# Attention and a routed layer on one core: rows of ten units by transposing DMAs, and a new written order

## Chip, cores, metric

The kernel runs on one core of a Trainium2 chip. The metric is the device time in microseconds (us) of one execution.

## What is computed

```python
scores = (1.0 / np.sqrt(64)) * np.matmul(q, k.transpose(0, 1, 3, 2))   # q, k, v: 8 x 12 x 448 x 64
attn = np.maximum(scores, 0.0) ** 2 / 448
x = np.matmul(attn, v)                    # then heads side by side: 8 x 448 x 768
for b in range(8):
    s = x[b] @ w_gate                     # one score for each of 448 rows
    top = np.argpartition(-s, 128)[:128]  # the 128 rows with the highest scores
    h = np.maximum(x[b, top] @ w1, 0.0)   # 768 x 1024
    out[b] = x[b]
    out[b, top] += (1.0 / (1.0 + np.exp(-s[top])))[:, None] * (h @ w2)
```

## The kernel before

The attention is cut into 24 units, each with four heads of one batch; three units make a batch (unit u belongs to batch u // 3). The engines are PE (TensorE, matrix products), ACT (ScalarE), DVE (VectorE), POOL (GpSimd, which here mainly issues DMAs) and SP (which issues the first loads and the transposing DMAs).

A unit goes through these steps. `L` (line 106) loads q, k and v of the unit with a cast to bf16, from POOL, into one of six buffers each. `T` (226) turns queries (w=0) and keys (w=1) on PE, and `TE` (240) copies them out of PSUM on DVE. `SC`, called `S` in the order (256), makes the scores of one of seven blocks of keys in a pair of PSUM banks; `R` (264) clamps them at zero on ACT into `r_sb`; `Q` (270) squares three or four blocks at once on DVE into `a_sb`. `V` (276) multiplies with the values over the seven blocks, and `X` (286) copies the result, scaled, on ACT or DVE into `xT_sb`, which holds features on partitions and tokens along the row; three such buffers go round by batch. The rows of the output need the opposite layout. Two ways lead there:

- `RT` (298) turns a unit on PE, by eight matmuls of 128 columns of weights or, with by64=1, sixteen of 64, and `RE` (307) copies the turned rows from PSUM into `x_rows` on DVE or ACT.
- `XB` (314) has SP issue two DMAs that transpose from `xT_sb` straight into `x_rows`, each over 128 partitions. Units in the list `BYDMA` (45), 15 to 20, go this way. So that a block of 128 partitions holds two neighbouring heads, `L` loads these units by two DMAs of 64 partitions each for q, k and v (line 115), where other units have one DMA of 128 (line 111).

`ST` (324) stores a batch's `x_rows` to the output from POOL by two DMAs. It has to wait for all three units' rows, and what POOL issues after it waits behind it. Then the routed layer of the batch follows (class `Moe`, 337): scores by `colx` and `colE`, ranks by `bt`, `rk`, `cs0`, `cs` and `rank`, the choice by `hots`, `sel` and `sE`, a gather `XG` of the chosen rows by an indirect DMA on POOL, `XT` and `xeE` to turn them, `h` and `hE`, `y` and `yE` for the two products, `gs` and `sig` for the gate, and `ADD`, an accumulating indirect DMA on POOL. The last batch doesn't gather; `xe` takes its chosen rows by matmuls with `x_rows`. `bt` and the steps after it for one batch stand among the attention of later units.

The order of all work is a string written out by hand, `ORDER` (535 to 623). A loop (629) reads it item by item and calls the function of that name; an item such as `R,0,3,A` is block 3 of unit 0 on ACT. Every engine gets its instructions in this order and runs them in this order, each engine as far ahead as its semaphores let it.

At the start, SP loads the first queries and keys in fp32 (`LFq`, `LFk`), ACT and DVE cast them (`Cq`, `Ck`), PE turns the first seven blocks of queries into one PSUM bank and the first two blocks of keys into the next, and `TQE` and `TKE` copy them out. `PW` is a matmul on zeros that only keeps PE occupied.

```python
def XB(u):
    for g in range(2):
        m = 2 * uu + g
        nc.sync.dma_start_transpose(out=x_rows[b][:, :, 128 * m:128 * m + 128],
                                    in_=xT_sb[b % NX][:, m].rearrange("p c n -> p (c n)"))
```

Of the kernel before, what the change touches and what calls it, by code (L numbers as in the profile page):

```python
# [678 lines left out]
```

## Time and profile before

| what | value |
|---|---|
| median of 3 runs | 197.46 us (197.3 to 199.45) |
| profiled execution, its own time | 197.49 us |
| its span, first to last instruction | 195.8 us |
| time outside the span | 1.69 us |
| TensorE clock granted, mean over the span | 0.986 of full |

Busy time counts what an engine executes; shares are of the span. A matmul's end is modelled in the profile, so a PE that looks busy can still be held up a little. An engine's idle time is put down to what ended it. SP's own instructions and DMA issues are not counted as busy there.

### The profile page before, as it was taken

The page shows a single profiled execution, that of the slowest core. Times are in us where ns is not written, and L with a number is a line of the kernel's source. Part 1 is how long each engine was busy: PE and PEld are TensorE (multiplying, and loading weights), DVE is VectorE, ACT ScalarE, POOL GpSimd, SP SyncE. Part 2 cuts the span into 40 slices and gives each one's busy share as a digit, 9 for nine tenths or more (in the row PEclk, how much of TensorE's full clock was granted, in tenths as well). Part 3 has the DMA queues.
Part 4 walks back from the last instruction along what each step waited for, and adds up shares of the span by engine and source line. Part 5 has one row for each costly group of instructions (what it writes and reads, how often), then busy time and mean ns, then how long its engine had stood idle before and what let it go on. Part 6 is the DMA issues. An engine that isn't in the chain of part 4 may idle for free.

```text
span 195.8 us, 7321 instructions
## 1 busy us (share of the span) xinstructions
PE 178.4 (91%) x3221; PEld 125.0 (64%) x3221; DVE 162.0 (83%) x228; ACT 164.4 (84%) x209; POOL 111.1 (57%) x160
## 2 busy tenths in 40 slices
PE   7888979989999999999999989999999999999900
PEld 7545647656667676775768765677667668588700
DVE  1599999999999999999999989897997969773100
ACT  4699999999999998899999989999998886533410
POOL 7958562558735189485794987229013367423360
PEclk9999999999999999999999999999999999999995
DMA  5999999999999969999999999998999999939391
GB/s 171 148 186 203 204 209 202 263 282 194 181 197 347 207 99 172 197 299 246 174 167 191 326 149 235 252 130 115 120 133 309 155 272 216 187 79 291 47 125 26
DMA packets 32333, 37.70 MB, mean 193 GB/s; under 512 B 8744, under 2 KB 29614, under 8 KB 31278
## 3 DMA queue, kind: packets, MB, share of 16 engines
q0 software_dynamic: 24928, 34.74, 95.4%
q1 hardware_dynamic: 7374, 2.50, 10.2%
q8 instruction: 25, 0.41, 0.9%
q14 instruction: 6, 0.05, 0.1%
HBM read 42.08 MB, written 14.16 MB: 287 GB/s over the span
## 4 chain that ended last, share of the span: by engine, by line
PE 61%; ACT 25%; issue 5%; DVE 4%; POOL 2%; POOLq 0%; DVEq 0%; ACTq 0%
ACT r_sb L216 24%; PE ps L260 12%; PE ps L487 10%; PE ps L505 10%; PE ps L281 9%; PE ps L233 7%; PE ps L295 4%; PE ps L209 2%; PE ps L365 2%; POOL out_dram L523 2%; PE ps L377 1%; DVE a_sb L274 1%; ACT xT_sb L216 1%; DVE qkt L220 1%; DVE mask_sb L388 1%
## 5 line engine op out<-in xcount | busy, mean ns | idle before, releaser
L216 ACT ACTIVATE r_sb<-ps 128x896 bf16<-128x896 f32 x168 | 140.2, 967 | 6.3 <-PE ps L260 5.8
L274 DVE TENSOR_TENSOR a_sb<-r_sb 128x2688 bf16<-128x2688 bf16 (+1 forms) x48 | 84.8, 1784 | 2.7 <-ACT r_sb L216 1.8
L260 PE MATMUL ps<-qkt 64*64 64x448 bf16 x672 | 55.5, 361 | 3.2 <-ACT r_sb L216 2.3
L281 PE MATMUL ps<-a_sb,v_sb 64*64 64x448 bf16 x672 | 41.7, 350 | 0.6 <-ACT r_sb L216 0.4
L260 PEld LDWEIGHTS <-qkt 64*64 64x64 bf16 x672 | 22.1, 104 | 21.1 <-issue 11.0
L220 DVE COPY qkt<-ps 128x1792 bf16<-128x1792 bf16 (+2 forms) x25 | 26.0, 1045 | 2.1 <-PE ps L233 1.6
L281 PEld LDWEIGHTS <-v_sb 64*64 64x64 bf16 x672 | 21.4, 107 | 9.3 <-issue 1.6
L446 POOL DMA_INDIRECT xg<-out_dram,idx x7 | 13.3, 1897 | 22.3 <-DVE idx L430 12.0
L487 PE MATMUL ps<-xeT,w_sb 128*128 128x128 bf16 (+1 forms) x396 | 24.6, 220 | 0.0
L487 PEld LDWEIGHTS <-w_sb 128*128 128x128 bf16 (+1 forms) x396 | 21.9, 98 | 4.0 <-issue 3.1
L505 PE MATMUL ps<-w_sb,hT 128*128 128x384 bf16 (+1 forms) x132 | 24.3, 327 | 0.0
L523 POOL DMA_INDIRECT out_dram<-gye,idx x9 | 17.4, 1929 | 8.6 <-ACT gye L216 6.6
L327 POOL DMA_DIRECT2D out_dram<-x_rows x8 | 4.5, 561 | 28.9 <-DMA x_rows<-xT_sb 9.2
L111 POOL DMA_DIRECT2D v_sb<-in_v_dram x18 | 14.0, 781 | 4.2 <-PE ps L260 1.8
L505 PEld LDWEIGHTS <-hT 128*128 128x128 bf16 (+1 forms) x132 | 11.1, 98 | 8.0 <-issue 2.1
L233 PE MATMUL ps<-ident,q_sb 128*64 128x128 bf16 x336 | 14.3, 225 | 1.6 <-ACT r_sb L216 1.2
L233 PEld LDWEIGHTS <-q_sb 128*64 128x64 bf16 x336 | 11.8, 112 | 6.3 <-issue 5.6
L222 DVE TENSOR_SCALAR xT_sb<-ps 128x896 bf16<-128x896 f32 x12 | 13.1, 1088 | 2.1 <-PE ps L281 1.2
L111 POOL DMA_DIRECT2D q_sb<-in_q_dram x17 | 12.9, 757 | 3.0 <-DVE a_sb L274 1.2
L233 PE MATMUL ps<-ident,k_sb 128*64 128x128 bf16 x336 | 14.1, 221 | 0.0
L111 POOL DMA_DIRECT2D k_sb<-in_k_dram x17 | 12.6, 741 | 2.2 <-PE ps L260 1.4
L216 ACT ACTIVATE xT_sb<-ps 128x896 bf16<-128x896 f32 x12 | 11.7, 975 | 0.8 <-PE ps L281 0.8
(122 smaller groups left out, 200.4 us busy)
## 6 DMA issues: line engine op xcount, KB each, us to landing
out_dram<-x_rows POOLq DMA_DIRECT2D x8, 768.0 KB, 5.5
out_dram<-x_rows POOLq DMA_DIRECT2D x8, 576.0 KB, 6.6
v_sb<-in_v_dram POOLq DMA_DIRECT2D x18, 224.0 KB, 8.2
q_sb<-in_q_dram POOLq DMA_DIRECT2D x17, 224.0 KB, 9.0
k_sb<-in_k_dram POOLq DMA_DIRECT2D x17, 224.0 KB, 8.7
w_sb<-in_moe_w_dram POOLq DMA_DIRECT2D x6, 256.0 KB, 8.2
w_sb<-in_moe_w_dram POOLq DMA_DIRECT2D x8, 192.0 KB, 8.0
q_sb<-in_q_dram POOLq DMA_DIRECT2D x12, 112.0 KB, 6.2
```

The lines of the kernel that those rows point to most:

```text
L111: nc.gpsimd.dma_start(out=dst, in_=src(t, u))
L216: nc.scalar.activation(out=out_, in_=in_, func=func or AF.Copy, scale=scale)
L220: nc.vector.tensor_copy(out=out_, in_=in_)
L222: nc.vector.tensor_scalar(out=out_, in0=in_, scalar1=scale, scalar2=None, op0=ALU.mult)
L233: nc.tensor.matmul(out=PSB[HALF[j], at["T", u, w], n * 128:(n + 1) * 128], lhsT=s[:, j, c, :], rhs=ident, is_transpose=True, start=(n == 0 ...
L260: nc.tensor.matmul(out=PS[HALF[hf], bank + j, :S], lhsT=qkt[u][HALF[j], 1, c, hf, :], rhs=qkt[u][HALF[j], 0, :, hf, :], start=True, stop=True)
L274: nc.vector.tensor_tensor(out=a_sb[u][:, c0:c1], in0=r, in1=r, op=ALU.mult)
L281: nc.tensor.matmul(out=PS[HALF[j], at["V", u] + hf, :S], lhsT=v_sb[u % NBUF][HALF[hf], j, c, :], rhs=a_sb[u][HALF[hf], c, j, :], start=(c ...
L446: read = reads[self.b] = nc.gpsimd.indirect_dma_start(out=self.xg, out_offset=None, in_=out[0:self.b + 1].rearrange("b s d -> (b s) d"), i ...
L487: nc.tensor.matmul(out=PS[p, self.at["h"] + bk, o:o + 128], lhsT=w1_sb[:, m, f * 128 + p.start:f * 128 + p.stop], rhs=self.xeT[:, m, :], s ...
L505: nc.tensor.matmul(out=PS[p, self.at["y"] + w, :384], lhsT=self.hT[:, f, p], rhs=w2_sb[:, f, w * 384:(w + 1) * 384], start=(f == 0), stop= ...
L523: add = nc.gpsimd.indirect_dma_start(out=out[0:self.b + 1].rearrange("b s (w d) -> (b s w) d", w=w), out_offset=bass.IndirectOffsetOnAxis( ...
```

## The change

The units whose rows go by transposing DMAs are now ten: 21 and 22 in the old manner, by two DMAs over 128 partitions behind loads in halves (`BYDMA`), and 9, 10, 12, 13, 15, 16, 18 and 19 (`BYFOUR`) behind whole loads, by four DMAs over 64 partitions each, one for each head. Units 17 and 20 go back to PE, so `RT` and `RE` remain for 14 units where there were 18. The first five blocks of the first queries go to one PSUM bank and the last two (`TB`) to another; their copies are split between ACT (five) and DVE (two), and DVE also copies the first keys. The order string is written anew in full; steps `X`, `hE`, `xeE` and `yE` change engines in places, and `PW,7` becomes `PW,5`.

```diff
-    BYDMA = (15,16,17,18,19,20)
+    BYDMA = (21,22)
+    BYFOUR = (9,10,12,13,15,16,18,19)
+    NA = 5
...
+        if (u, w, n0) == (0, 0, 0):
+            n1 = NA
+        o = NA if (u, w, n0) == (0, 0, NA) else 0
...
+    def TB(bank):
+        at["TB"] = bank
+        T(0, 0, bank, NA, NC)
...
         for g in range(2):
             m = 2 * uu + g
-            nc.sync.dma_start_transpose(
-                out=x_rows[b][:, :, 128 * m:128 * m + 128],
-                in_=xT_sb[b % NX][:, m].rearrange("p c n -> p (c n)"))
+            if u in BYDMA:
+                nc.sync.dma_start_transpose(
+                    out=x_rows[b][:, :, 128 * m:128 * m + 128],
+                    in_=xT_sb[b % NX][:, m].rearrange("p c n -> p (c n)"))
+                continue
+            for j in range(2):
+                h = 4 * uu + 2 * j + g
+                nc.sync.dma_start_transpose(
+                    out=x_rows[b][:, :, 64 * h:64 * h + 64],
+                    in_=xT_sb[b % NX][HALF[j], m].rearrange("p c n -> p (c n)"))
...
-    Zz PW,32,0 Zi Zs LFq Cq,0 Zt LFk,0,2 Zm Ck,0,2,D Cq,1 T,0,0,0 TK,0,2 LFk,2,7 TQE,0,7,D Ck,2,7,D TKE,0,2,A
+    LFq Zz PW,32,0 Zi Zs Zh Cq,1 Zt Cq,0 T,0,0,0 TB,2 LFk,0,2 Ck,0,2,D TK,0,2 TQE,5,7,D LFk,2,7 TKE,0,2,D
+    TQE,0,5,A PW,5,3 S,0,0,2 S,0,1,4 R,0,0,A Ck,2,7,D R,0,1,A TK,2,7 Lw TKE,2,7,D Zm PW,8,6 S,0,2,0 R,0,2,A
```

SP's queue, before: all six units' transposes behind the first loads.

```order
L320 DMA_TRANSPOSE x_rows<-xT_sb_105 128x4x128 [waits DMASW4_49,DMASW5_49,DVE_49,Pool_49]
L320 DMA_TRANSPOSE x_rows<-xT_sb_105 128x4x128
L320 DMA_TRANSPOSE x_rows<-xT_sb_105 128x4x128 [waits DMAHW0_49,Activation_49]
L320 DMA_TRANSPOSE x_rows<-xT_sb_105 128x4x128 [waits DMAHW1_49]
L320 DMA_TRANSPOSE x_rows<-xT_sb_105 128x4x128 [waits DMAHW2_49,DVE_49]
L320 DMA_TRANSPOSE x_rows<-xT_sb_105 128x4x128 [waits DMAHW3_49]
```

SP's queue now, the first two units (10, then 9, both of batch 3 in the first `xT_sb` buffer).

```order
L339 DMA_TRANSPOSE x_rows_2089<-xT_sb0_103 128x4x64 [waits DMASW6_49,DMASW7_49,DVE_49,Pool_49]
L339 DMA_TRANSPOSE x_rows_2089<-xT_sb0_103 128x4x64
L339 DMA_TRANSPOSE x_rows_2089<-xT_sb0_103 128x4x64 [waits DMAHW0_49]
L339 DMA_TRANSPOSE x_rows_2089<-xT_sb0_103 128x4x64 [waits DMAHW1_49]
L339 DMA_TRANSPOSE x_rows_2089<-xT_sb0_103 128x4x64 [waits DMAHW2_49,Activation_49]
L339 DMA_TRANSPOSE x_rows_2089<-xT_sb0_103 128x4x64 [waits DMAHW3_49]
L339 DMA_TRANSPOSE x_rows_2089<-xT_sb0_103 128x4x64 [waits DMAHW4_49]
L339 DMA_TRANSPOSE x_rows_2089<-xT_sb0_103 128x4x64 [waits DMAHW5_49]
```

Twelve transposing DMAs in SP's queue have become thirty-six, 32 of them half as large, and they begin six units earlier.

POOL's queue around the store of batch 6 (two DMAs from `x_rows`) and the load of the last values, unit 23's (`v_sb_102`), before.

```order
L327 DMA out_dram<-x_rows 64x3072
L328 DMA out_dram<-x_rows 64x2304
L523 DMA out_dram<-gye,idx 1344x768
L111 DMA v_sb_102<-in_v_dram 128x2x448
L523 DMA out_dram<-gye,idx 1792x768
```

The same place now; `v_sb_100` and `v_sb_101` are the values of units 21 and 22.

```order
L117 DMA v_sb_100<-in_v_dram 64x2x448 x2
L117 DMA v_sb_101<-in_v_dram 64x2x448 x2
L465 DMA xg<-out_dram,idx 128x768
L346 DMA out_dram<-x_rows 64x3072
L347 DMA out_dram<-x_rows 64x2304
L113 DMA v_sb_102<-in_v_dram 128x2x448
```

The accumulating DMA that stood between the store and the load has moved behind; the load is still behind the store.

ACT's queue from the last `r_sb` evictions on, before (`hT`, `xeT`, `gye` are written by `hE`, `xeE`, `yE`).

```order
L216 ACTIVATE r_sb<-ps 128x896 x7
L216 ACTIVATE x_rows<-ps 128x4x256
L479 ACTIVATE g__3045<-ps 128x1
L216 ACTIVATE r_sb<-ps 128x896 x4
L216 ACTIVATE x_rows<-ps 128x4x256
L216 ACTIVATE xT_sb_104<-ps 128x2x448
L216 ACTIVATE x_rows<-ps 128x4x256
L216 ACTIVATE hT<-ps 128x1024
```

ACT's queue at the same place now.

```order
L218 ACTIVATE gye<-ps,g__2482 128x768
L218 ACTIVATE r_sb<-ps 128x896 x6
L218 ACTIVATE xT_sb_104<-ps 128x2x448
L218 ACTIVATE hT<-ps 128x1024
L218 ACTIVATE xT_sb_104<-ps 128x2x448
L218 ACTIVATE x_rows<-ps 128x4x256
```

Two of the three copies into `x_rows` (units 21 and 22) have left ACT's end; a copy into `xT_sb` and one into `hT` have come to it.

## Rows read from the trace of the kernel before

**Rows 1.** The page, part 1: busy time, share of the span, instructions.

```profile
PE 178.4 (91%) x3221; PEld 125.0 (64%) x3221; DVE 162.0 (83%) x228; ACT 164.4 (84%) x209; POOL 111.1 (57%) x160
```

**Rows 2.** Busy time by stretch: PE, PEld, DVE, ACT, POOL, granted clock, DMA share, GB/s.

```profile
10.00:70.00 60.00, 54.82 (x1062) 36.40 (x1057) 58.73 (x77) 60.00 (x75) 33.48 (x51) 1.00 1.19 222
70.00:160.00 90.00, 89.04 (x1670) 62.08 (x1667) 82.95 (x117) 85.10 (x109) 53.74 (x72) 1.00 1.15 194
160.00:186.50 26.50, 26.26 (x388) 19.93 (x385) 16.33 (x28) 13.16 (x20) 12.04 (x14) 1.00 0.77 174
```

**Rows 3.** Waits: who waited for whom, us in total, times, longest.

```profile
POOL out_dram L327 <- DMA x_rows<-xT_sb: 9.2, 1, 9.2
```

**Rows 4.** The chain that ended last: start, us, what.

```profile
73.44 0.55 PE ps L295 x8
74.00 1.30 PE ps L505 x8
...
112.52 0.47 PE ps L295 x16
...
169.81 1.48 PE ps L281 x28
...
180.50 1.34 PE ps L487 x24
```

**Rows 5.** Groups by line and shape, evictions on DVE and ACT: busy us, mean ns.

```profile
L220 DVE COPY x_rows<-ps 128x1024 bf16<-128x1024 bf16 x14 | 9.5, 684 | 0.3 <-issue 0.2
...
L216 ACT ACTIVATE xT_sb<-ps 128x896 bf16<-128x896 f32 x12 | 11.7, 975 | 0.8 <-PE ps L281 0.8
...
L216 ACT ACTIVATE x_rows<-ps 128x1024 bf16<-128x1024 bf16 x4 | 4.2, 1051 | 2.7 <-PE ps L295 2.7
...
L216 ACT ACTIVATE hT<-ps 128x1024 bf16<-128x1024 f32 x3 | 3.1, 1026 | 2.3 <-PE ps L487 2.3
...
L216 ACT ACTIVATE xeT<-ps 128x768 bf16<-128x768 bf16 x3 | 2.6, 871 | 0.0
...
L216 ACT ACTIVATE gye<-ps,g__743 128x768 f32<-128x768 f32 x1 | 0.9, 901 | 0.2 <-PE ps L505 0.2
```

**Rows 6.** Instructions on the tile x_rows: ns min/median/max, first and last start.

```profile
L320 SPq DMA_TRANSPOSE x_rows<-xT_sb x12: 1190/1276/3841, 126.0 to 154.0; - x12
```

**Rows 7.** The transposing line alone: DMA to landing.

```profile
DMA to landing us min/median/max: 3.5/4.8/9.0
```

**Rows 8.** DMA queues from 125 to 160 us: packets, MB, share of 16 engines.

```profile
q1 hardware_dynamic: 6528, 1.57, 48.1%
```

**Rows 9.** DMA issues of the whole span: count, KB each, median us to landing.

```profile
q_sb<-in_q_dram POOLq DMA_DIRECT2D x17, 224.0 KB, 9.0
...
q_sb<-in_q_dram POOLq DMA_DIRECT2D x12, 112.0 KB, 6.2
```

**Rows 10.** Groups by line on POOL: whole loads (L111) and halves (L115).

```profile
L111 POOL DMA_DIRECT2D q_sb<-in_q_dram x17 | 12.9, 757 | 3.0 <-DVE a_sb L274 1.2 <-DMA q_sb<-in_q_dram 0.8 <-PE ps L260 0.6
...
L115 POOL DMA_DIRECT2D q_sb<-in_q_dram x12 | 7.4, 635 | 0.8 <-issue 0.8
```

**Rows 11.** Timeline of the start: start us, us, what.

```profile
5.70 0.62 DVE L220 COPY qkt<-ps 128x896 bf16<-128x896 bf16 x1 [0.40 <-PE ps L233]
...
5.91 0.38 ACT L216 ACTIVATE qkt<-ps 128x256 bf16<-128x256 bf16 x1 [1.26 <-PE ps L233]
...
6.81 7.53 ACT L216 ACTIVATE r_sb<-ps 128x896 bf16<-128x896 f32 x9 [0.51 <-PE ps L260]
```

**Rows 12.** Timeline from 160 us on: last values, last r_sb, weights of last V, last DMA.

```profile
160.66 1.43 POOL L111 DMA_DIRECT2D v_sb<-in_v_dram  x1
...
164.71 3.35 ACT L216 ACTIVATE r_sb<-ps 128x896 bf16<-128x896 f32 x4 [1.62 <-PE ps L260]
...
169.74 1.12 PEld L281 LDWEIGHTS <-v_sb 64*64 64x64 bf16 x28 [0.37 <-issue]
...
188.08 1.56 POOL L523 DMA_INDIRECT out_dram<-gye,idx  x1 [0.26 <-issue]
```

More of the change, by code (lines that the diff above doesn't have):

```diff
@@ L232, in T @@
             for j in range(2):
-                nc.tensor.matmul(out=PSB[HALF[j], at["T", u, w], n * 128:(n + 1) * 128],
+                nc.tensor.matmul(out=PSB[HALF[j], bank if o else at["T", u, w], (n - o) * 128:(n - o + 1) * 128],
                                  lhsT=s[:, j, c, :], rhs=ident, is_transpose=True,
-                                 start=(n == 0), stop=(n == NC - 1), skip_group_check=True)
+                                 start=(n == o), stop=(n == n1 - 1 if (u, w) == (0, 0) else n == NC - 1),
+                                 skip_group_check=True)
+    def TB(bank):
+        at["TB"] = bank
+        T(0, 0, bank, NA, NC)
     def TK(n0, n1):
@@ L247, in TE @@
         else:
-            put(eng, flat[:, w, n0 * 128:n1 * 128], PSB[:, at["T", u, w], n0 * 128:n1 * 128])
+            own = (u, w, n0) == (0, 0, NA)
+            put(eng, flat[:, w, n0 * 128:n1 * 128],
+                PSB[:, at["TB"], :(n1 - n0) * 128] if own else PSB[:, at["T", u, w], n0 * 128:n1 * 128])
     def TQE(n0, n1, eng):
@@ L621 @@
[L621 to L622 removed]
+    LFq Zz PW,32,0 Zi Zs Zh Cq,1 Zt Cq,0 T,0,0,0 TB,2 LFk,0,2 Ck,0,2,D TK,0,2 TQE,5,7,D LFk,2,7 TKE,0,2,D
+    TQE,0,5,A PW,5,3 S,0,0,2 S,0,1,4 R,0,0,A Ck,2,7,D R,0,1,A TK,2,7 Lw TKE,2,7,D Zm PW,8,6 S,0,2,0 R,0,2,A
+    L,q,1 Zc S,0,3,2 S,0,4,6 S,0,5,4 L,k,1 Q,0,0,3 R,0,3,A R,0,4,A L,k,2 T,1,0,0 T,1,1 S,0,6,2 Zg,6 R,0,5,A
@@ new lines @@
+    W,1,3,8 V,8,5 V,8,6 X,8,A W,1,2,8 T,11,0,6 T,11,1 TE,11,2,D Zx,2 RT,6,1,2 R,10,3,A S,10,4,0 colx,2,0,3
+    colx,2,1 RE,6,D colx,2,2 colE,2 S,10,5,4 R,10,4,A W,1,6,8 S,10,6,6 S,11,0,2 W,1,1,8 R,10,5,A R,10,6,A
+    Q,9,0,3 sel,1,0 sE,1 RT,7,0,1 RE,7,D RT,8,0,4 bt,2,5 rk,2,0 RE,8,D rk,2,2 S,11,1,6 V,9,0,0 V,9,1 ST,1
+    W,1,7,8 V,9,2 R,11,0,A L,q,13 S,11,2,2 R,11,1,A V,9,3 V,9,4 V,9,5 V,9,6 R,11,2,A rk,2,3 y,0,0,2,0,6
+    y,0,1,2,0 L,k,13 rk,2,1 W,1,5,8 X,9,A S,11,3,2 R,11,3,A S,11,4,4 y,0,2,2,0 y,0,3,2,0 L,v,10 L,v,11 S,11,5,0
@@ new lines @@
+    h,1,7,0 S,13,2,4 V,11,0,6 hE,1,2,D V,11,1 S,13,3,2 V,11,2 V,11,3 V,11,4 R,13,2,A V,11,5 R,13,3,A S,13,4,0
+    R,13,4,A L,k,15 Q,12,3,7 S,13,5,4 V,11,6 X,11,A L,q,14 T,14,0,2 T,14,1 TE,14,2,D R,13,5,A y,1,0,2,1,0
+    y,1,1,2,1 y,1,2,2,1 S,13,6,6 L,v,13 Q,13,0,3 L,q,16 S,14,0,2 S,14,1,4 XB,10 y,1,3,2,0 y,1,4,2,0 R,13,6,A
+    Q,13,3,7 y,1,5,2,0 R,14,0,A y,1,6,2,0 colx,3,0,6 colx,3,1 colx,3,2 R,14,1,A gs,1,7 sig,1 L,q,15 S,14,2,2
+    R,14,2,A T,15,0,4 T,15,1 colE,3 S,14,3,6 TE,15,2,D RT,11,0,2 RE,11,D y,1,7,2,0 L,q,18 R,14,3,A bt,3,3 rk,3,3
@@ new lines @@
+    T,19,1 TE,19,2,D S,18,5,6 S,18,6,0 L,k,20 h,3,4,0 h,3,5,0 R,18,5,A h,3,6,0 h,3,7,0 R,18,6,A Q,18,3,7
+    V,17,0,6 V,17,1 V,17,2 S,19,0,0 S,19,1,4 V,17,3 V,17,4 hE,3,2,A R,19,0,A R,19,1,A S,19,2,2 R,19,2,A V,17,5
+    V,17,6 XB,15 T,20,0,0 T,20,1 X,17,D TE,20,2,D S,19,3,4 R,19,3,A S,19,4,6 colx,5,0,2 R,19,4,A colx,5,1
+    colx,5,2 sel,4,3 L,q,21 colE,5 S,20,0,0 sE,4 Q,19,0,3 S,20,1,4 bt,5,2 rk,5,2 rk,5,0 gs,3,3 R,20,0,A R,20,1,A
+    V,18,0,6 V,18,1 S,20,2,0 V,18,2 V,18,3 V,18,4 V,18,5 V,18,6 RT,17,0,4 cs0,5,5 R,20,2,A ST,4 XB,16 rk,5,1
```

158 lines of the change are left out of this document (71 added, 87 removed).

## Prediction

> **What bounds the kernel now.** I read the busy shares first, then the same by stretch, then the chain that ended last and the waits, and last the timelines of the two ends. The shares [rows 1] give PE 91%, ACT 84% and DVE 83%: no engine alone explains the time. By stretch [rows 2] they do. From 10 to 70 us ACT is busy 60.00 of 60 us, while PE has 5 us free: ACT sets the pace. From 70 to 160 us PE is busy 89.04 of 90, with ACT close behind at 85.10, so PE sets the pace and ACT has 4.9 us to spare. From 160 to 186.5 us PE is busy 26.26 of 26.5 and ACT only half the time: PE alone. [...] After PE's end there remain the last accumulating DMA, issued at 188.08 [rows 12], and its landing. DMA shares are above 1 because queues overlap, and the transfers are not what PE waits for; the one long wait on them is POOL's, 9.2 us once, for transposed rows before a store [rows 3].
>
> The profiled execution took 197.49 us against a median of 197.46, so sums made on its trace need no correction. About 1% (2 us) is what a measurement of this kernel can tell from no change.
>
> **The change part by part.**
>
> *Turns on PE.* By the order string, 18 turns become 14: of those with by64=0 13 become 10, of those with by64=1 five become four. A turn costs 0.55 us on the chain in the first form and 0.47 in the second [rows 4]. PE sheds 3 x 0.55 + 0.47 = 2.1 us. All six units that leave PE (9, 10, 12, 13, 21, 22) and both that come back (17, 20) lie behind 70 us, where PE sets the pace.
>
> *Evictions.* Counted in the two strings, ACT loses three copies to `x_rows` (3 x 1.05), three to `xeT` (3 x 0.87), and half a `gye` (0.6); it gains an `xT_sb` (0.98), two and a half `hT` (2.6) and three `gye` (3 x 0.90) [rows 5], and some 0.5 at the start and in the last `xeT`. That is 6.3 lost, 6.8 gained: +0.5 us, spread over the span, which I count at nothing. DVE sheds the other side of these moves and one copy to `x_rows` (0.68), some 6 us in all, but it bounds no stretch, so I count that at nothing.
>
> *The stretch where ACT sets the pace.* It ends near 75 us, within unit 10. The 77th `r_sb` eviction (unit 10's last) stood behind five copies to `xT_sb`; now it stands behind four and a gate of 0.2 us. That is worth 0.8 us there, if DVE, busy 58.73 of 60 us [rows 2], takes the copy without being late. Ends: 0.8 gained; or, DVE having nearly no room, nothing or some loss: a copy more of about 1.1 us on DVE, delaying the squares by that much. I take 0, in the middle.
>
> *Start.* The first scores wait for two copies in parallel, 896 columns on DVE (0.62 us, from 5.70) and 256 on ACT (0.38, from 5.91) [rows 11]. Now ACT takes 640 and DVE two of 256. ACT's need not wait for the keys' turn any more, DVE's second still does. The last to end should be DVE's, at about 5.91 plus less than 0.38, so near 6.2 instead of 6.32: 0.15 us earlier. Ends: 0.4 earlier, or 0.3 later, should ACT's 640 columns wait for the same matmuls as today and then take as long as DVE's 896. I take -0.15.
>
> *Loads.* 36 half loads become 12 and 52 whole loads become 64 on POOL: 24 x 0.635 - 12 x 0.757 = 6.2 us of POOL's time less [rows 10]. POOL is busy 57% of the span, so this shortens nothing by itself; it lets a load behind others start earlier. Bytes are the same.
>
> *Transposing DMAs.* In the 35 us from 125 on, the twelve took 48.1% of 16 engines [rows 8]: 16.8 us, or 1.40 us each, for 128 partitions of 1 KB. No row shows one of 64 partitions. Lower bound: half, as its bytes are half, so 4 x 1.40 + 32 x 0.70 = 28.0 us, 11.2 more. Upper bound: the same 1.40, 50.4 us, 33.6 more. Spread over some 85 us from unit 10's result on, that is 0.13 to 0.40 on top of a DMA share of 1.15 [rows 2]. I take the lower end: the packets in the queue's row (6528 for 12, 544 each) fit a count by 256 B of source, which halves with the partitions. On SP an issue takes 1.28 us [rows 6]; a unit's four take 5.1 where two took 2.6, and its rows are ready 3 x 1.28 + 4.8 = 8.6 us after `X`, by the median landing [rows 7], against 6.1 before. Behind unit 10's four stand unit 9's, which is ready earlier but is issued second; batch 3's store waits for both, about 14 us behind unit 10's `X`. Behind that store on POOL are the values of units 15 and 18, wanted five units later and more. I count it as hidden.
>
> [...]
>
> *Where it could bite.* The last values, unit 23's, are loaded behind batch 6's store on POOL, before and now. Before, the load went out at 160.66; with the 9.0 us of a whole load [rows 9] it lands at 169.7, and `V` of unit 23 begins at 169.74, its first weights behind a gap of 0.37 us [rows 12]: already just in time. Now the store waits for unit 19's four transposes. From unit 19's `X`: 3 x 1.28 = 3.8, the last landing 4.8, two stores' issue 1.1, the load 9.0: 18.7 us. PE's work in between by the string: 21 block steps of `V` and 18 of `S` (some 0.2 each, from 28 matmuls in 1.48 us [rows 4]), 16 groups of `h` (0.34), 8 of `y` (0.33), four `T`, five `colx`, a turn and small ones (another 4.5): near 21 us. So it is covered by about 2 us.
>
> *The end.* Behind the last `r_sb` eviction, which ended at 164.71 + 3.35 = 168.06 [rows 12], PE loses unit 22's turn (0.5) but gets four groups of `h` (1.3), four of `y` (1.3) and two gate rows of the last batch (0.4) that stood before it: 2.5 us heavier. PE has 2.1 + 2.5 = 4.6 us less before it. On ACT, before it, two copies to `x_rows` and three to `xeT` go, one `hT`, two `gye` and the start's 0.3 come: 4.7 - 3.1 = 1.6 us less. So the last eviction can come 4.6 us earlier as far as PE goes, and 1.6 plus part of ACT's spare 4.9 us as far as ACT goes.
>
> *Sum.* PE alone gives -2.1. But in the stretch before 160 us ACT hands PE its data block by block with 95% of its own time taken and no work lost, so part of what PE gains comes back as waits for `r_sb`. Ends of what is kept: all, 2.1; or none and 0.9 lost (third rival). I take half, 1.05. With the start: 197.49 - 1.05 - 0.15 = 196.3 us.
>
> **The rivals.**
>
> *All of it is kept, and the first stretch too.* PE works without a gap from 70 us on, the order fits, ACT's 0.8 us counts, and the earlier last load does no harm: 197.49 - 2.1 - 0.8 - 0.15 = 194.4. For it: PE's 98.9% from 70 to 160 [rows 2], and 6 us less on both POOL and DVE. Against it: ACT's total is unchanged.
>
> *Slower: the transposes come late.* If a DMA over 64 partitions costs 1.40 us like one over 128, unit 19's last landing rises towards the longest of today, 9.0 [rows 7], and the whole load's 9.0 with it. The mechanism is the chain above: transposes, store on POOL, last values, `V` of unit 23, with PE waiting in order behind it. It decides from a landing of about 4.8 + 2 = 7 us on; at 9.0 and a load of 12 it is 4.2 + 3 - 2 = 5 us late, one for one in the end: 196.3 + 5 = 201.3; half of it, 198.8, if only half of these two delays comes. I price it at 200.5. For it: POOL's 9.2 us wait for just such rows [rows 3]. Against it: half the bytes.
> [...]
>
> *ACT holds the end.* PE's relief before the last `r_sb` eviction is not used, ACT brings it 1.6 us earlier and no more, and the 2.5 us of added tail follow in full: 197.49 + 2.5 - 1.6 = 198.4. For it: ACT's 95%. Against it: ACT's spare time there came from waiting for PE, which now has less to do.
>
> **How the numbers follow.** Chances: forecast 0.40 (195.0 to 197.6 of its own); all kept 0.30; transposes late 0.17; ACT holds the end 0.13. Faster by over 1% (under 195.5): most of the second, 0.28, and a quarter of the first, 0.10: 0.38. Slower by over 1% (above 199.4): most of the transposes' case, 0.14, and of ACT's case and others 0.06: 0.20. Within 1%: 0.42. The range leaves 0.1 on each side: down to 193.2, somewhat under the second case, and up to 200.6, the price of the slower one.
>
> **What would show it.** Right: no PE wait for DMAs; transposes in the queue's row at about 0.7 us of 16 engines each; PE's turns fewer by 2.1 us on the chain; the last `r_sb` eviction between 164 and 166 us; `V` of unit 23 without a wait on `v_sb`; first `r_sb` at 6.65. Wrong: a transpose's landing above 7 us in the middle, PE idle ahead of unit 23's `V`, a last `r_sb` eviction later than 166.4, or ACT busy under 58 us between 10 and 70, which would mean that the new order makes it wait.

## The result, and the profile after

The changed kernel took 200.12 us in the middle of 16 runs (197.88 to 204.44), the kernel before 197.42 beside it. The ratio is 1.011, 95% interval 1.008 to 1.0141: slower by 1.1%. Forecast was 196.3; the time lies at the upper end of the range, on the wrong side of no change. Middles are of all runs, ratios of the undisturbed ones alone, and since a gap of the kind found below can by itself put a run among the disturbed, both are given. The profiled execution took 200.34 us (span 198.3).

From the page of the changed kernel: busy time (the line to [rows 1]), PE's and its granted clock's tenths in 40 slices, the queues of transposes and of instructions, the transposes' landing:

```profile
PE 178.3 (90%) x3219; PEld 123.9 (62%) x3219; DVE 155.6 (78%) x225; ACT 165.8 (84%) x209; POOL 98.5 (50%) x148
...
PE   7888999879999999999999989999999599999910
...
PEclk9999999999999999999999999999999979999985
...
q1 hardware_dynamic: 12238, 3.55, 15.5%
q8 instruction: 25, 0.41, 0.9%
...
x_rows<-xT_sb SPq DMA_TRANSPOSE x36, 7.0
```

By stretch (columns as in [rows 2]):

```profile
10.00:70.00 60.00, 54.83 (x1086) 36.85 (x1080) 58.45 (x68) 59.77 (x76) 34.54 (x54) 1.00 1.19 220
70.00:160.00 90.00, 86.29 (x1600) 59.61 (x1599) 80.34 (x111) 83.48 (x103) 38.90 (x52) 0.99 1.23 197
160.00:189.00 29.00, 29.00 (x432) 21.17 (x429) 12.18 (x29) 16.60 (x24) 12.91 (x16) 0.97 0.97 193
```

The first stretch is as before. In the second PE is idle for 3.7 us where it was idle for 1.0, and 2.2 of it stand in one slice of the page (the 5, at 154 to 159 us); the clock falls in the next one. PE's timeline there (start, us, what, and in brackets the idle time ahead and what ended it):

```profile
155.53 0.38 PE L396 MATMUL ps<-ident_f,cols 128*128 128x128 f32 x2
158.10 0.58 PE L396 MATMUL ps<-ident_f,cols 128*128 128x128 f32 x2 [2.19 <-issue]
```

and the two stretches, of the gap and behind it:

```profile
155.80:158.10 2.30, 0.11 (x1) 0.00 (x0) 0.17 (x1) 0.86 (x2) 1.08 (x1) 1.00 1.33 138
158.10:161.60 3.50, 3.50 (x26) 1.73 (x26) 1.71 (x8) 1.10 (x3) 0.00 (x0) 0.51 0.96 159
```

PE stands still for 2.2 us in the middle of four like matmuls (`bt` of batch 6), and "issue" says that it waited for nothing that the profile shows. In the kernel before the same four run on end (0.63 us):

```profile
153.56 0.63 PE L377 MATMUL ps<-ident_f,cols 128*128 128x128 f32 x4
```

Over the 3.5 us behind the gap the granted clock is 0.51 in the mean, in the gap itself 1.00; the trace's clock record has it at half of full speed for 3.4 us from 158.13 on. Eight score matmuls take 0.96 us there, and 0.57 in the kernel before, where the clock at that place was 1.00:

```profile
160.03 0.96 PE L272 MATMUL ps<-qkt 64*64 64x448 bf16 x8
```

```profile
155.13 0.57 PE L260 MATMUL ps<-qkt 64*64 64x448 bf16 x8
```

The rest of the chain: the last `r_sb` eviction, the last values' `V` (28 matmuls, no wait in brackets, as forecast) and the last accumulating DMA:

```profile
165.77 2.58 ACT L218 ACTIVATE r_sb<-ps 128x896 bf16<-128x896 f32 x3
```

```profile
170.83 1.52 PE L293 MATMUL ps<-a_sb,v_sb 64*64 64x448 bf16 x28
```

```profile
190.88 1.56 POOL L542 DMA_INDIRECT out_dram<-gye,idx  x1 [0.26 <-issue]
```

The last `r_sb` ends at 168.35, before at 168.06 [rows 12]; unit 21's last one had still been ahead by 1.66 us (149.64 against 151.30). From the last `r_sb` to the last DMA it is 22.5 us, before 20.0: the tail is 2.5 us heavier.

The chain of the slower rival did start. POOL waited for transposing DMAs ahead of a store twice, 15.3 us in all, the second time 5.1 us for unit 19's ahead of batch 6's store; that went out at 162.0 us (before 158.2) and the last values' load at 163.1 (before 160.7). PE, itself late, did not wait for them.

```profile
  POOL out_dram L346: 15.3, 2
```

```profile
162.02 0.57 POOL L346 DMA_DIRECT2D out_dram<-x_rows  x1 [5.14 <-issue]
...
163.09 0.76 POOL L113 DMA_DIRECT2D v_sb<-in_v_dram  x1
```

**What the gap is.** The page has a queue q8 of the kind "instruction": 25 packets, 0.41 MB, so 16 KB each. PE's records hold 6438 matmuls and weight loads, so one packet comes for some 256 of them. No view lists the packets singly; what follows is counted from the records of the traces (weight loads and matmuls in order of time, two instructions a pair, packets from 0). No packet starts before PE has passed some 150 to 180 places of its 256, and every gap sits at 170 to 188 places of the next 256: by these counts the packets are PE's own instructions, 256 in each, and PE seems to ask for a packet when it enters the one ahead, and needs it when that one ends. That is a reading of the counts; the asking itself is in no record: "asked for" below is the moment at which PE passes place 180, and a packet is as late as its start lies behind that. Packet 20 was asked for at 149.4 us, started only at 155.57 and landed at 156.47; PE stood from instruction 5560 (21 x 256 + 184) on until 158.10. In the kernel before the same packet started 1.05 us after it was asked for.

### The profile page after: what moved, and what is told of

Same layout as the page of the kernel before. It is cut to its first block, busy times and chain, and to the rows that moved or that the text cites. A ratio compares the mean times of both kernels' runs of the same rounds, so it can differ in the third digit from the quotient of the medians.

```text
span 198.3 us, 7363 instructions
## 1 busy us (share of the span) xinstructions
PE 178.3 (90%) x3219; PEld 123.9 (62%) x3219; DVE 155.6 (78%) x225; ACT 165.8 (84%) x209; POOL 98.5 (50%) x148
## 3 DMA queue, kind: packets, MB, share of 16 engines
q1 hardware_dynamic: 12238, 3.55, 15.5%
## 4 chain that ended last, share of the span: by engine, by line
PE 57%; ACT 20%; DVE 9%; issue 8%; POOL 2%; POOLq 0%; ACTq 0%; DVEq 0%
ACT r_sb L218 19%; PE ps L272 12%; PE ps L506 10%; PE ps L524 10%; PE ps L293 9%; PE ps L238 6%; DVE a_sb L286 3%; PE ps L307 2%; PE ps L211 2%; PE ps L384 2%; DVE qkt L222 2%; POOL out_dram L542 2%; PE ps L396 1%; DVE xT_sb L224 1%; ACT xT_sb L218 1%
## 5 line engine op out<-in xcount | busy, mean ns | idle before, releaser
L272 PE MATMUL ps<-qkt 64*64 64x448 bf16 x672 | 56.5, 363 | 4.2 <-ACT r_sb L218 1.5
L293 PE MATMUL ps<-a_sb,v_sb 64*64 64x448 bf16 x672 | 43.1, 351 | 1.3 <-issue 0.6
L272 PEld LDWEIGHTS <-qkt 64*64 64x64 bf16 x672 | 23.2, 104 | 21.4 <-issue 10.7
L524 PE MATMUL ps<-w_sb,hT 128*128 128x384 bf16 (+1 forms) x148 | 25.6, 334 | 0.1
L465 POOL DMA_INDIRECT xg<-out_dram,idx x7 | 7.6, 1085 | 34.3 <-DVE idx L449 17.0
L542 POOL DMA_INDIRECT out_dram<-gye,idx x9 | 15.2, 1684 | 9.4 <-ACT gye L218 7.7
L113 POOL DMA_DIRECT2D k_sb<-in_k_dram x21 | 15.6, 747 | 5.1 <-PE ps L272 2.5
L113 POOL DMA_DIRECT2D q_sb<-in_q_dram x21 | 15.9, 762 | 3.0 <-PE ps L272 1.2
L113 POOL DMA_DIRECT2D v_sb<-in_v_dram x22 | 16.3, 750 | 2.0 <-issue 0.7
L407 DVE SCALAR_TENSOR_TENSOR mask_sb<-ps,cols,tie 128x448 bf16<-128x448 f32 (+2 forms) x24 | 12.3, 546 | 3.5 <-PE ps L396 2.8
```

Of the source, the lines that this page charges most:

```text
L113: nc.gpsimd.dma_start(out=dst, in_=src(t, u))
L272: nc.tensor.matmul(out=PS[HALF[hf], bank + j, :S], lhsT=qkt[u][HALF[j], 1, c, hf, :], rhs=qkt[u][HALF[j], 0, :, hf, :], start=True, stop=True)
L293: nc.tensor.matmul(out=PS[HALF[j], at["V", u] + hf, :S], lhsT=v_sb[u % NBUF][HALF[hf], j, c, :], rhs=a_sb[u][HALF[hf], c, j, :], start=(c ...
L407: nc.vector.scalar_tensor_tensor(out=mask, in0=row[:, o:S], scalar=self.cols[:, c:c + 1], in1=tie[:, :S - o], op0=ALU.subtract, op1=ALU.is ...
L465: read = reads[self.b] = nc.gpsimd.indirect_dma_start(out=self.xg, out_offset=None, in_=out[0:self.b + 1].rearrange("b s d -> (b s) d"), i ...
L524: nc.tensor.matmul(out=PS[p, self.at["y"] + w, :384], lhsT=self.hT[:, f, p], rhs=w2_sb[:, f, w * 384:(w + 1) * 384], start=(f == 0), stop= ...
```

## Experiments

All times are against the kernel before in the same series. "Profiled" is the time of the execution that was profiled, which can lie far from the middle. Gaps are those above 1 us between two weight loads of PE at a packet's end, in that execution, with the packet that PE waited for in brackets; the changed kernel's own, above, is 2.3 us (20) by this measure.

| run | edit of | middle (lowest to highest), us | before | ratio [95%] | profiled, us | gaps, us (packet) |
|---|---|---|---|---|---|---|
| `again` | after, none | 200.14 (197.98 to 202.0) | 197.19 | 1.011 [1.006, 1.016] | 197.98 | 1.3 (20) |
| `ph_plus` | after | 202.17 (200.5 to 204.57) | 197.19 | 1.024 [1.020, 1.028] | 201.94 | 1.1 (8), 2.3 (20) |
| `ph_minus` | after | 200.33 (196.99 to 203.62) | 197.19 | 1.004 [1.001, 1.008] | 200.53 | 1.3 (19) |
| `bydma` | after | 202.95 (198.78 to 216.63) | 197.19 | none | 202.12 | 1.4 (8), 1.5 (19), 2.8 (20) |
| `no_t` | after | 196.79 (196.32 to 197.2) | 197.14 | 0.998 [0.996, 1.000] | 196.32 | none |
| `v22late` | after | 201.03 (199.42 to 203.02) | 197.14 | 1.016 [1.012, 1.020] | 200.25 | 2.7 (20) |
| `vearly` | after | 202.34 (198.69 to 205.36) | 197.14 | 1.012 [1.007, 1.018] | 198.69 | 1.2 (14), 1.8 (20) |
| `v23` | after | 202.27 (200.58 to 206.39) | 197.14 | 1.022 [1.018, 1.026] | 201.29 | 3.2 (20) |
| `before_plus` | before | 198.54 (197.42 to 199.34) | 197.92 | 1.001 [0.998, 1.005] | 197.50 | none |
| `by2` | after | 201.15 (199.02 to 204.65) | 197.92 | 1.008 [1.004, 1.013] | 202.94 | 2.4 (14), 1.1 (20) |
| `pe19` | after | 199.72 (198.01 to 205.56) | 197.92 | 1.004 [1.000, 1.008] | 205.56 | 4.2 (19) |
| `swap` | after | 201.79 (198.76 to 206.69) | 197.92 | 1.012 [1.007, 1.016] | 201.87 | 1.2 (14), 1.5 (17) |
| `copy` | after | 198.06 (197.12 to 200.05) | 197.87 | 1.001 [0.998, 1.004] | 197.38 | none |
| `before_dense` | before | 198.12 (197.36 to 199.41) | 197.87 | 1.000 [0.997, 1.002] | 199.41 | 1.2 (14) |
| `cand` | after | 199.31 (198.11 to 201.02) | 197.87 | 1.006 [1.003, 1.009] | 201.02 | 1.2 (14) |
| `thin` | after | 203.17 (200.91 to 205.1) | 197.87 | 1.022 [1.016, 1.027] | 203.15 | 1.1 (20) |

### Is it the instruction stream?

`again`: no edit.

> The changed kernel, unaltered, for a second look. In its first profile PE stood still from 155.91 to 158.10 us in the middle of the four matmuls at L396 with nothing to wait for, and its clock was then at the lower level until 161.5; the instruction packet fetched at 155.57 for PE was the latest of all, counted in PE instructions. Theory F (PE ran out of instructions because that packet came late, and the stand-still then cost the clock): the same gap at the same instructions, 1.5 to 3 us long, again with the packet starting at about 155 us; time 199.5 to 200.5. Theory O (the new order itself costs the time, through its heavier tail; the stand-still was chance): no gap over 1 us in this profile, and a time of 199.5 to 200.5 all the same. If the gap is missing and the time is near 197 to 198, the event is there in some executions and not in others, and F holds for the difference.

`ph_plus` and `ph_minus` cut or join the warm-up matmuls, so that everything behind them changes its place in the stream, and their columns in all nearly stay (6976 and 7041, against 7040; in `ph_plus` they take 5.3 us of PE, in the changed kernel 5.4):

```diff
-    def PW(n, bank):
+    def PW(n, bank, w):
-            nc.tensor.matmul(out=PS[:, bank, :128], lhsT=zero, rhs=zero, ...
+            nc.tensor.matmul(out=PS[:, bank, :w], lhsT=zero[:, :128], rhs=zero[:, :w], ...
-  PW,32,0      PW,5,3      PW,8,6      PW,10,7
+  PW,48,0,84   PW,10,3,64  PW,16,6,64  PW,20,7,64     (ph_plus)
+  PW,8,0,512   PW,2,3,320  PW,2,6,512  PW,3,7,427     (ph_minus)
```

> The changed kernel with its 55 warm-up matmuls before 12 us cut into 94 shorter ones of the same time in all (32 of 128 columns into 48 of 84, 23 of 128 into 46 of 64): nothing else moves, but every later instruction of PE stands 78 places later in its stream, so each packet of 256 instructions begins 78 instructions earlier in the work. Theory F: packet 20 is asked for about 2 us earlier in the work, ahead of the loads issued from 146.2 us on, and the gap at L396 goes or changes place; time 196 to 198 if no other packet comes late. Theories O and D: no change, 199.5 to 200.5, and a gap, if there is one, at the same matmuls.

> The other way: the 55 warm-up matmuls of 128 columns joined into 15 longer ones of the same time in all, so that every later instruction of PE stands 80 places earlier in its stream and each packet begins 80 instructions later in the work. Theory F: the gap at L396 goes or moves by some 80 instructions; if the packet still starts at 155.6 us, PE is then 358 instructions into the packet before and not 438, and does not run dry: 196 to 198. Theories O and D: no change, 199.5 to 200.5, and a gap, if there is one, at the same matmuls.

PE's timelines around the gap, of `again`:

```profile
155.57 0.38 PE L396 MATMUL ps<-ident_f,cols 128*128 128x128 f32 x2
157.08 0.38 PE L396 MATMUL ps<-ident_f,cols 128*128 128x128 f32 x2 [1.13 <-issue]
```

of `ph_plus`:

```profile
154.30 0.44 PE L307 MATMUL ps<-ident,xT_sb 128*128 128x128 bf16 x5
156.90 0.33 PE L307 MATMUL ps<-ident,xT_sb 128*128 128x128 bf16 x3 [2.16 <-issue]
```

and of `ph_minus`:

```profile
151.10 0.64 PE L506 MATMUL ps<-xeT,w_sb 128*64 128x128 bf16 x16
152.94 0.41 PE L506 MATMUL ps<-xeT,w_sb 128*64 128x128 bf16 x8 [1.21 <-issue]
```

The work at the gap is another each time (gate rows, a turn, the hidden layer), the place in the stream is not. Counted from the records:

| kernel | gap at PE's instruction | packet: asked for, start, landed | PE goes on |
|---|---|---|---|
| after | 5560 = 21 x 256 + 184 | 149.4, 155.57, 156.47 | 158.10 |
| `again` | 5560 | 149.4, 154.26, 155.64 | 157.08 |
| `ph_plus` | 5560 | 149.1, 154.46, 155.35 | 156.90 |
| `ph_minus` | 5304 = 20 x 256 + 184 | 145.0, 150.35, 151.37 | 152.94 |
| `no_t` | none | 149.2, 152.56, 153.45 | |

So theory F is shown in its main point: PE stops where a packet ends, with the next one not yet landed, and goes on 1.4 to 1.6 us after it has. Its guess at the times was off: a shift did not free the kernel, it moved the gap or added one (`ph_plus` has a second at 70.6 us), since packets asked for at 145.0, 149.1 and 149.4 us all came 4.8 us late or more. `again` gives the cost: beside the first profile it has 1.06 us less of a gap and no stretch at the lower clock behind it (granted from 156 to 160 us: 1.00 against 0.77; PE busy 177.0 against 178.3 us), 2.4 us in all, which is the 197.98 against 200.34. That execution was the fastest of its six; what those of 200 us and more had that were not profiled, no trace shows. Theory O falls with the next run.

### What makes the packet late?

`no_t` leaves the eight transposing DMAs of units 18 and 19 out:

```diff
     def XB(u):
+        if u in (18, 19):
+            nc.vector.memset(x_rows[b][:, :, 256 * uu:256 * uu + 256], 0.0)
+            return
```

> The changed kernel without the eight transposing DMAs of units 18 and 19: their part of the result's rows is zeros from VectorE instead, so that part of the output is left out. Nothing else moves. Theory T (the transposes share the DMA engines with the loads, which are then served late, and PE's packet 20, asked for near 149.4 us, stands behind that backlog): the packet starts less than 4 us after it is asked for (4.8 and 6.2 in the two profiles so far), no gap of PE at the boundary 256 times 21 plus 184, and 195.5 to 197 us. Theory V (the four half loads of the values of 21 and 22, stacked behind batch 5's store, are what it waits for): the gap stays, 1 us or more, and 198 to 200.5 us.

In the other three a load of values moves in the order string:

```diff
-  ... ST,5 ADD,1 ... L,v,22 rk,6,2 ... XG,5 ...
+  ... ST,5 ADD,1 ... rk,6,2 ... XG,5 L,v,22 ...               (v22late)
-  ... ST,5 ADD,1 ... L,v,21 ... L,v,22 ...
+  ... L,v,21 L,v,22 ST,5 ADD,1 ...                            (vearly)
-  ... XG,5 ... ST,6 ... g,7,2 L,v,23 ...
+  ... XG,5 L,v,23 ... ST,6 ... g,7,2 ...                      (v23)
```

> The changed kernel with the load of unit 22's values issued after batch 5's gather instead of behind batch 5's store, so some 8 us later, and 224 KB less stand in the DMA queues when packet 20 is asked for. Theory V: the packet comes 1 to 2 us earlier, the gap falls to under 1 us, 196.5 to 198 us. Theory T: the packet starts still over 4 us after it is asked for, 198.5 to 200.5 us. If the values themselves come late, PE waits for them ahead of unit 22's values and the gap has only changed its place.

> The changed kernel with the loads of the values of units 21 and 22 issued ahead of batch 5's store instead of behind it, at a place where GpSimd waited 4 us: near 139.8 instead of 146.2 us. If what delays packet 20 is the sum of what stands in the queues (theories T and V in one), nothing changes, since the bytes ahead of it are the same: a gap of 1 us or more and 199 to 200.5 us. If the DMA engines had room between 140 and 149 us, the packet comes in time and the time is 196 to 198 us.

> The changed kernel with the last values' load (unit 23) issued right after batch 5's gather, ahead of batch 6's store, near 157 us instead of 163. Theory L (the rival of the prediction: late transposes hold batch 6's store, and the last values behind it): the executions in which PE waited for these values are gone, the time falls by 1 us or more in the middle and the slowest, above 201 us, are gone. Theory F (instruction fetch alone): gap and middle as before, 199.5 to 200.5 us.

`no_t`, PE's timeline over the same four matmuls (three lines lower in this file), its last `r_sb` evictions and its last DMA:

```profile
155.39 0.60 PE L399 MATMUL ps<-ident_f,cols 128*128 128x128 f32 x4
```

```profile
159.53 4.98 ACT L218 ACTIVATE r_sb<-ps 128x896 bf16<-128x896 f32 x6
```

```profile
187.06 1.56 POOL L545 DMA_INDIRECT out_dram<-gye,idx  x1 [0.27 <-issue]
```

All four matmuls run on end; the last `r_sb` ends at 164.51 and the last DMA goes out 1.0 us earlier than before. No run was above 197.2. Theory T holds for packet 20: without these eight DMAs it is 3.3 us late, the gap is gone, and the order is no longer slower than the kernel before (0.35 us under it in the middle, the ratio's interval reaching 1.000; 1.2 us had been forecast). Theory V falls: with 224 KB less in the queues packet 20 came 7.2 us late, with the loads moved ahead 5.3. Theory L falls as the main cause: with the last values loaded at 157.5 us, ahead of batch 6's store, PE has no wait for them, and the time is still 2.2% above the kernel before. That the gap was the longest there is not this edit's doing: packet 20 had started at 156.60 us, ahead of the moved load, so gaps of 1.3 (`again`), 2.3 and 3.2 us are the spread of one and the same order up to that place. In single executions the last values do cost time (see 'Why the prediction was wrong'). In `v22late` the DMA engines moved next to nothing ahead of that packet (windows; the last figure is GB/s, 46 and 20 in the first two):

```profile
148.00:150.00 2.00, 2.00 (x42) 1.62 (x43) 1.98 (x3) 2.00 (x4) 0.64 (x2) 1.00 0.47 46
150.00:152.00 2.00, 2.00 (x58) 1.41 (x52) 2.00 (x2) 2.00 (x4) 0.00 (x0) 1.00 0.07 20
152.00:154.00 2.00, 1.69 (x51) 1.43 (x45) 1.11 (x2) 1.85 (x3) 0.00 (x0) 1.00 0.90 335
```

and in `no_t` not:

```profile
148.00:150.00 2.00, 1.96 (x40) 1.37 (x41) 1.94 (x4) 2.00 (x3) 0.60 (x2) 1.00 1.05 163
150.00:152.00 2.00, 2.00 (x62) 1.55 (x56) 2.00 (x2) 2.00 (x4) 1.18 (x1) 1.00 1.12 181
```

By the records 15 packets of batch 5's store (12 KB each), in flight together, took 3.8 to 5.4 us there, in the changed kernel 2.1 to 2.3, in `v23` 2.8 to 4.3 and in `by2` 2.8 to 3.1; in `no_t`, `again` and the kernel before such packets took at most 1.1. That adds to the delay, but is not all of it: `again`, `vearly` and `ph_plus` have gaps of 1.3, 1.8 and 2.3 us without it.

### Is it the split into four, the bytes, or the turning?

`bydma` gives all eight units, `by2` only units 18 and 19, two DMAs over 128 partitions and half loads:

```diff
-    BYDMA = (21,22)
-    BYFOUR = (9,10,12,13,15,16,18,19)
+    BYDMA = (9,10,12,13,15,16,18,19,21,22)     (bydma)
+    BYFOUR = ()
+    BYDMA = (18,19,21,22)                      (by2)
+    BYFOUR = (9,10,12,13,15,16)
```

> The order of the changed kernel, but its eight units 9, 10, 12, 13, 15, 16, 18 and 19 as units 21 and 22 are: loads in two halves, two transposing DMAs over 128 partitions each: 20 transposes where there were 36, and 24 half loads more of POOL's issue. Theory D (the four transposes over 64 partitions each clog the DMA queues, and make packets late): the gap goes, transposes land in 5 us in the middle, time 196.0 to 197.5, as the forecast said of the order. Theory F with the burst of loads as its cause: the gap stays or moves, 199 to 200.5. Theory O: 199.5 to 200.5 without a gap.

> The changed kernel with units 18 and 19 alone by two transposing DMAs over 128 partitions each instead of four over 64 (and so by loads in halves). Theory T in its wide form (any transposing DMA there makes packet 20 late): the gap at its boundary stays, 1 to 3 us, 199.5 to 202 us. Theory D (it is the split into four): the gap is under 0.9 us, 196.5 to 198 us.

`copy` moves the same 512 KB by four plain DMAs:

```diff
+            if u in (18, 19):
+                nc.sync.dma_start(out=x_rows[b][:, :, 128 * m:128 * m + 128], in_=xT_sb[b % NX][:, m])
+                continue
```

> The changed kernel with the eight transposing DMAs of units 18 and 19 replaced by four plain DMAs, on the same queue of SyncE, that copy the same 512 KB untransposed into the same rows: so those rows of the output are not turned. Theory B (bytes and descriptors on the DMA engines make packet 20 late): the gap at its boundary stays, 1 to 3 us, 198.5 to 201 us. Theory X (it is the transposing itself, with nothing else at fault): no gap over 0.9 us there, 196.3 to 197.5 us, as without these DMAs.

Theory D falls: with two DMAs over 128 partitions the gaps stay, 2.8 us at packet 20 in `bydma` and 1.1 in `by2`, whose longer one (2.4) is at packet 14. Nor was `bydma`, with 20 transposes over 128 partitions where the changed kernel has 32 over 64 and four over 128, the faster one in the middle of its runs: 202.95 us, against the 200.14 of `again` in the same series. `copy` speaks for theory X: packet 20 comes after 3.3 us, as in `no_t`, no gap above 0.8 us, 197.38 us in the profile; the middle of its runs lies between the two theories' times, the ratio with 1.001 at that of the kernel before. Yet its copies hold the engines nearly as long. The page's rows of `copy`, and the queue's row of `no_t`:

```profile
q1 hardware_dynamic: 12046, 3.55, 15.1%
...
x_rows<-xT_sb SPq DMA_TRANSPOSE x28, 7.3
...
x_rows<-xT_sb SPq DMA_DIRECT2D x4, 128.0 KB, 8.8
```

```profile
q1 hardware_dynamic: 9934, 3.02, 11.9%
```

Over their spans that is 29.5 us of 16 engines in `copy`, 23.2 in `no_t` and 30.7 in the changed kernel: some 6.4 us for the four copies, 7.6 for the eight transposes. So the engines' time is hardly all that these transposes take. But the copies were also issued sooner: unit 19's two by 146.7 us, its four transposes from 146.1 to 151.3. No run separates the turning from this timing, so what in these transposes makes others wait stays open. Some runs of `copy` reach 200.05; what they had no trace shows.

### Why is the kernel before spared?

It turns units 15 to 20 by DMA at the same time. `before_plus` shifts its stream by 114 places, `before_dense` puts two loads among its transposes:

```diff
-        for _ in range(n):
-            nc.tensor.matmul(out=PS[:, bank, :128], lhsT=zero, rhs=zero, ...
+        for _ in range(2 * n):
+            nc.tensor.matmul(out=PS[:, bank, :64], lhsT=zero, rhs=zero[:, :64], ...      (before_plus)
-  ... ST,5 ... XG,5 ... L,v,22 ... ST,6 ... L,v,23 ...
+  ... L,v,22 L,v,23 ST,5 ... XG,5 ... ST,6 ...                                           (before_dense)
```

> The kernel before, with each of its 57 warm-up matmuls of 128 columns (all before 12 us) made two of 64 columns: the same time in all, and every later instruction of PE stands 114 places later in its stream, so each packet is asked for some 3.3 us earlier in the work. Nothing else moves. Theory P (the kernel before ran without the gap only because its packets were asked for at times when the DMA queues had just drained: at 149.2 us it came after 1.05 us): packet 19 is now asked for near 140 us, when loads and transposes fill the queues until 145.8, and comes 4.5 to 5.8 us later; PE stands still 0.8 to 2.5 us at its boundary, near 145 us, and the time is 198.3 to 201. Rival (the gap belongs to the order or the transposes of the changed kernel): 197.0 to 197.6, no gap over 1 us.

> The kernel before, with the last two loads of values (units 22 and 23) issued ahead of batch 5's store, where GpSimd waited 9.2 us for transposed rows, at about 137 us instead of 155.8 and 160.7. Theory O (the overlap: transposes do harm only where loads run beside them, and the kernel before was spared since its loads stood behind that wait): packet 19, asked for near 143 us, comes over 4 us late instead of 2.6, PE has a gap of over 0.8 us at its boundary near 149 us, and the time is 198.3 to 200.5. Rival (transposes over 128 partitions with loads in halves are harmless in any company): no gap, 196.5 to 197.6.

Theory P falls: with every packet asked for at another time none came more than 4.2 us late, and there is no gap. Theory O of `before_dense` (the overlap with loads; not the O above) is half right: packets 19 and 20 came 3.75 and 4.36 us late instead of 2.6 and 1.05, but PE was not yet through with the packet ahead, and the time did not change. Its gap of 1.2 us is at packet 14, where the kernel before has one of 0.8. `thin` asked whether PE's pace decides: it goes through the 256 instructions in question in 6.1 us in the changed kernel and in some 7.8 before.

```diff
-  colx,6,0,6 RT,20,0,7 RE,20,D colx,6,1 ... yE,4,2,A S,23,1,0
+  colx,6,0,6 colx,6,1 ... yE,4,2,A RT,20,0,7 RE,20,D S,23,1,0
```

> The changed kernel with unit 20's turn (16 of PE's short instructions) and its copy moved from ahead of batch 4's last matrix products to behind them, out of the 256 instructions that PE goes through while packet 20 is under way. Theory S (the gap comes where PE goes through 256 instructions in less time than a late packet takes: 6.1 us in the changed kernel, 7.8 in the kernel before at the same packet): longer instructions take the place of these, the 256 take about 7.2 us, the gap shrinks by about 1 us against those of 1.3 to 3.2 seen so far, and the time is 197.5 to 199.3 us. If only the delay of the packet mattered: gap and time as before, 199.5 to 201 us. If unit 20's rows then hold batch 6's store and the last values, PE waits for those near 169 us and the gain is gone.

It settles nothing: a gap of 1.1 us stayed. The new place made waits of its own (the third case named there), 1.2 us on ACT ahead of the turn and 1.0 ahead of the last values; two more on DMAs, 1.0 for gathered rows at 145.4 us and 0.8 for `k_sb` at 154.1, lie ahead of it. The first two:

```profile
162.97 0.61 PE L307 MATMUL ps<-ident,xT_sb 128*128 128x128 bf16 x8 [1.17 <-ACT gye L218]
172.97 1.52 PE L293 MATMUL ps<-a_sb,v_sb 64*64 64x448 bf16 x28 [1.03 <-DMA v_sb<-in_v_dram]
```

So why the kernel before is spared stays open.

### Three versions that keep the output

```diff
-  ... XB,19 y,4,0,2,0,6 ...
+  ... RT,19,0,7 RE,19,D y,4,0,2,0,6 ...                                    (pe19)
-  ... RT,20,0,7 RE,20,D ... XB,19 ... XG,5 ... L,v,23
+  ... RT,19,0,7 RE,19,D ... XB,20 ... XG,5 L,v,23 ...                      (swap)
-  XB,18 ... RT,20,0,7 RE,20,D ... XB,19 ... XG,5 ... L,v,23
+  ... RT,18,0,7 RE,18,D ... RT,19,0,7 RE,19,D XB,20 ... XG,5 L,v,23 ...    (cand)
```

> The changed kernel with unit 19 turned by PE (a turn in PSUM bank 7 and a copy by VectorE at the place where its transposing DMAs stood): four transposes fewer, and some 0.6 us more on PE, 0.7 on VectorE. Theory T: packet 20 comes between the 3.3 us of the kernel without both units' transposes and the 4.8 to 7.3 of those with both, say 4 us, the gap is under 1 us; 197 to 198.5 us. Theories without the transposes: gap as before, 200 to 202 us.

> The changed kernel with units 19 and 20 exchanged: 19 turned by PE at the place of 20, and 20 by four transposing DMAs, issued some 5 us later than those of 19; and the last values' load right after batch 5's gather, ahead of batch 6's store, which now has to wait for unit 20's rows until 162 to 166 us. PE's work is the same. Theory T: fewer transposes stand in the queues when packet 20 is asked for, the gap at its boundary shrinks below 1 us, 196.5 to 198 us, unless the next packet comes late in its place. Theories without the transposes: 200 to 202 us.

> A version that might beat both: the changed kernel with units 18 and 19 turned by PE (at the places of unit 20's turn and unit 19's transposes), unit 20 by four transposing DMAs instead, issued only from about 151 us on, and the last values' load ahead of batch 6's store. One turn more on PE, 0.55 us. By theory T no transpose stands in the queues when packets 19 and 20 are asked for: 197.0 to 197.8 us (196.8 without the transposes, and 0.55). If unit 20's transposes make packet 21 late, or hold the last store, 198.5 to 200.5.

None beats the kernel before, and all three miss the times that theory T gave them. With unit 19's transposes gone the long gap sat one packet earlier, at packet 19, which came 5.8 us late. That profile is of the slowest of `pe19`'s 13 executions (205.56 us); its ratio, 1.004, lies between those of `no_t` and the changed kernel. Its timeline:

```profile
150.53 0.74 PE L293 MATMUL ps<-a_sb,v_sb 64*64 64x448 bf16 x12
155.22 0.59 PE L272 MATMUL ps<-qkt 64*64 64x448 bf16 x4 [3.95 <-issue]
```

This is instruction 5304, 20 x 256 + 184; the packet landed at 151.09 and PE went on only 4.1 us later, which no record explains. In `swap` and `cand` the gaps sit at other packets (14 and 17 in the one, 14 in the other). These two also move the last values' load as `v23` does, which by itself had a ratio of 1.022 against the changed kernel's 1.011; beside `v23` they gain (1.012 and 1.006, in other series), as theory T would have it; against the changed kernel the two edits are not told apart. So the transposes of units 18 and 19 are what the time hangs on in this order, but turning them elsewhere was not enough in any version tried, and `no_t` leaves two units' rows out of the output.

## Why the prediction was wrong

- **The step that failed** is "I count it as hidden", of the transposing DMAs: their time was set against stores and loads, and PE's own instructions, which come by a DMA queue too, had no term in the sum. What the runs showed in its place: PE without instructions for 1.3 and 2.3 us in the two profiles of the changed kernel (up to 3.2 in its close variants), and where the clock fell some 1.3 us more, at a packet that comes 4.8 and 6.2 us after it is asked for (up to 7.3). Without the eight transposes of units 18 and 19 it is 3.3, and the time 196.8.
- *Transposes' cost on the engines*: right. 15.5% of 198.3 us less the 3.2 us of other DMAs on that queue (10.2% of 195.8 less 12 x 1.40) leaves 27.5 us, less 4 x 1.40, over 32: 0.69 us each, forecast 0.70. *Landing*: mis-sized. The sum had 4.8 us for all; the 32 over 64 partitions took 7.5 in the middle and up to 12.8, the four over 128 took 4.4, all together 7.0 by the page. The prediction called more than 7 a sign of being wrong.
- *The slower rival* gave 200.5, near the result, but by luck: its price was for another chain. The start of that chain came (landings of 7.5 us, batch 6's store held for 5.1), but in the profile the last values had no wait ahead of them, PE being late itself. It does bite in some executions: `ph_minus` waited 2.2 us there, `by2` 1.9, `thin` 1.0.
- *Turns, and half of the gain kept*: `no_t` gained 1.2 us in its profile (196.32 against the 197.49 of the profile before, another series), as forecast, but 0.35 in the middle of its own series, and its ratio reaches 1.000. In the changed kernel itself none of it was left.
- *The end*: right. 2.5 us heavier, in `again` as in `no_t` (22.55 us from the last `r_sb` to the last DMA in both, 20.0 before), and the last `r_sb` of `no_t` at 164.5, in the 164 to 166 of the forecast; in `again` 165.98, in the changed kernel's profile 168.35, later than the 166.4 that the prediction called a sign of being wrong.
- *Start*: right in sign; the first `r_sb` at 6.57 us (forecast 6.65, before 6.81), of which 0.06 is left at the end of unit 0. *ACT's stretch*: 59.77 of 60 busy, no wait, as forecast.
- The sum had no term for the clock. In the kernel before none was needed: 1.00 in all three stretches [rows 2]. In the changed kernel the granted clock behind the gap of 2.3 us was 0.51 in the mean from 158.1 to 161.6 us.

## What to carry to other kernels

Count an engine's own instructions among the customers of the DMA queues: PE, with 6438 matmuls and weight loads, took a packet of 16 KB every 5 to 10 us here, and it stood for 1.3 and 2.3 us in the two profiles of the changed kernel though the profile shows no operand that was late. By these traces it stops when the packet's delay, its transfer and the 1.4 us or so behind its landing are together longer than PE's work on the instructions ahead: in `again` 4.8 + 1.4 + 1.4 us against 6.4, and it stood for 1.3; in `no_t` 3.3 + 0.9 + some 1.4 against 6.2, and it did not; nor at packet 15 of the changed kernel, 4.9 us late with 9.7 us of work ahead. A stall marked "issue" in the middle of a row of like instructions is to be counted in instructions: if it sits at the same place of a packet in two kernels whose work differs there, as at 5560 and 5304 here, 256 apart, suspect the stream. Where DMA queues are full, price a new DMA also by what it does to the slowest packet (packet 20 was 4.8 and 6.2 us late with the eight transposes of units 18 and 19, 3.3 without), and test by leaving it out.
